# Strassen output products behind the attention: two interleaved groups of 192-column products, or one group of 384-column products per token pair

## The chip, the cores and the metric

One core of one Trainium2 chip. The metric is the device time of one execution in microseconds (us); the time before is the median of three runs. Engines are named as in the profile: PE (TensorE matmul), PEld (TensorE weight load), DVE (VectorE), ACT (ScalarE), POOL (GpSimd), SP (SyncE, which here only issues transfers).

## The reference

Softmax attention over 8 batches, 12 heads, 448 tokens and head size 64, followed by a SwiGLU block on the 3584 x 768 result:

```python
scores = scale * np.matmul(q, k.transpose(0, 1, 3, 2))
attn = np.exp(scores - np.max(scores, axis=-1, keepdims=True))
attn = attn / (np.sum(attn, axis=-1, keepdims=True) + 1e-09)
x = np.matmul(attn, v).transpose(0, 2, 1, 3).reshape(B * S, H * D)      # 3584 x 768
g = x @ w_gate                                                           # 768 x 1536
return (g * (1.0 / (1.0 + np.exp(-g))) * (x @ w_val)) @ w_out            # 1536 x 768
```

The change concerns only the last product, hidden (3584 x 1536) times w_out (1536 x 768).

## The kernel before

Everything is emitted in an order written out by hand. The attention runs over pairs of heads; the blocks of the SwiGLU (384 or 512 tokens of a pair of batches) are interleaved with it, so that PE always has something to do while ACT makes the exponentials. Behind the attention, from about 300 us on, PE alone sets the pace. What is left there is, in order of time: the gate and value products of a 512-token block by a seven-product (Strassen) scheme (`Unit`, L833); the output products of the three token pairs that are still open (`run_groups`, the groups named `og`, L710); the gate and value products of the last two batches, again by `Unit`, with the output of one odd 128-token chunk in between (`single_out`, L1039); and the output products of the last three token pairs (again `run_groups` and `og`, L710), with the stores that end the kernel.

**The output product of a token pair.** A token pair is 256 tokens, two chunks x and y of 128. Its hidden values have 12 chunks of 128 features, in two halves of NH = 6, so the left operand has four blocks: A11, A12 (chunk x) and A21, A22 (chunk y). The right operand is split into row halves and two column groups of equal width. Seven products of six matmuls each replace the eight of the plain form. Four sums of w_out's blocks (`Tsum`, made by `out_sums` on DVE during the attention) and four sums of the hidden blocks (`h_sums`, L571 to L574, four operations on DVE for each token pair) are operands.

In `out_group` the column groups are the two 192-column quarters of one 384-column half of w_out (`QW` = 192, `OH` = 384), so a token pair takes two groups, `qw` = 0 and 1, of seven products of 192 columns. The sums `Tsum` pair the same quarters. A group takes one tile of two PSUM banks from the pool `ps_s` (three such tiles; the pool `ps_f` has two tiles of one bank): `a` and `c` share the first bank and `b` has the second. The order of the seven products on PE is a, c, b, b, a, c, b:

1. `a` and `c` receive the first two products. Then ACT copies `a` to p1 (L756), and DVE makes p15 = c/HS + p1 (L757).
2. `b` receives the third product, and DVE writes c = HS * p15 + b (L759).
3. `b` receives the fourth, and DVE takes from it the right quarter of row y (`part`, L763).
4. `a` and `c` receive the fifth and sixth, and ACT copies both to row x in one operation of 384 columns (L735).
5. `b` receives the seventh, and DVE takes from it the left quarter of row y (L773).

The generator yields after step 2, and `run_groups` runs the two groups of a token pair interleaved: group one's first stage, group two's first stage, group one's second, group two's second. While one group's copies run, PE is in the other's products. `add_sum` takes the next waiting DVE operation from the list `sums`: four to a token pair, at places between the stages. The list holds `h_sums` of the next token pairs, and behind the first three pairs also `token_sums` (L1028 to L1031), four larger sums for the last `Unit` stage.

The two rows of a token pair are stored from SP's queue in parts (`store`, L671). The very last token pair stores in smaller parts as they become ready, from the queues of SP and ACT in turn.

Of the kernel before, what the change touches and what calls it, by code (L numbers as in the profile page):

```python
# [16 lines left out]
HS = 4096.0  # L17
# [48 lines left out]
def kernel(  # L66
# [487 lines left out]
    def out_sums(c):  # L554
        b11, b12, b21, b22 = (
            wo_all[:, :, ds(f, 2), ts(i, QW)].rearrange("p h c m -> p c h m") for f in (c, NH + c) for i in range(2)
        )
        t1, t2, t3, t4 = (t[:, ds(c, 2)].rearrange("p c (h m) -> p c h m", h=2) for t in Tsum)
        return [
            lambda: nc.vector.tensor_sub(t1, b12, b11),  # L560
            lambda: nc.vector.tensor_sub(t2, b22, t1),
            lambda: nc.vector.tensor_sub(t3, b22, b12),
            lambda: nc.vector.tensor_sub(t4, b21, t2),
        ]
# [137 lines left out]

    def out_group(kk, c0, hts, t, at, qw, osb, last=False, own=False, mid=None):
        x, y, w = ts(2 * t, 128), ts(2 * t + 1, 128), ts(qw, QW)
        g = ps_s.tile([128, 2, 512], FP32, tag="s", name="og")
        a, c, b = g[:, 0, 0:QW], g[:, 0, QW:OH], g[:, 1, 0:QW]

        def product(dst, lhs, rhs, first=False):
            return [
                nc.tensor.matmul(  # L710
                    dst, lhsT=lhs(n), rhs=rhs(n), start=first and n == 0, stop=n == NH - 1, skip_group_check=True
                )
                for n in range(NH)
            ]

        def hh(half, z):
            return lambda n: hts[:, half * NH + n, z]

        def hs(m):
            return lambda n: Hall[at][m][:, n]  # L720

        def bb(oh, half):
            return lambda n: wo[qw][:, half * NH + n, ts(oh, QW)]

        def tt(m):
            return lambda n: Tsum[m][:, n, w]

        def out_part(z, src):
            if last and qw:
                halves = [osb[z][:, ds(qw * OH + x * QW, QW)] for x in range(2)]  # L730
                return [
                    nc.scalar.activation(halves[0], src[:, 0:QW], AF.Copy, scale=1.0 / HS),
                    nc.vector.tensor_scalar_mul(halves[1], src[:, QW:], 1.0 / HS),
                ]
            return [nc.scalar.activation(osb[z][:, ts(qw, OH)], src, AF.Copy, scale=1.0 / HS)]  # L735

        def stored(z, lo=0, w=OH):
            l0 = c0 + (2 * t + z) * 128
            if last:
                store(osb[z], kk, l0, 128, qw * OH + lo, w, (nc.sync, nc.scalar), True)  # L740
            elif qw and not lo:
                store(osb[z], kk, l0, 128, 0, DM)

        def apart(mms, *others):
            for mm in mms:
                for other in others:
                    tc.declare_no_dep(mm.ins, other.ins, reason="another bank")

        product(a, hh(0, x), bb(0, 0), True)
        product(c, hh(0, y), tt(0))  # L750
        p1 = fp.tile([128, QW], FP32, tag="p1", name="p1")
        p15 = fp.tile([128, QW], FP32, tag="p15", name="p15")
        if own:
            keep1 = nc.vector.tensor_scalar_mul(p1[:], a, 1.0 / HS)
        else:
            keep1 = nc.scalar.activation(p1[:], a, AF.Copy, scale=1.0 / HS)  # L756
        keep15 = nc.vector.scalar_tensor_tensor(p15[:], c, 1.0 / HS, p1[:], ALU.mult, ALU.add)  # L757
        apart(product(b, hs(0), tt(1), True), keep1, keep15)
        nc.vector.scalar_tensor_tensor(c, p15[:], HS, b, ALU.mult, ALU.add)  # L759
        yield  # L760
        product(b, hs(1), tt(2))
        d = osb[1][:, ds(qw * OH + QW, QW)]
        part = nc.vector.scalar_tensor_tensor(d, b, 1.0 / HS, p15[:], ALU.mult, ALU.add)  # L763
        if last:
            stored(1, QW, QW)
        if mid:
            mid()
        apart(product(a, hh(1, x), bb(0, 1)), part)
        apart(product(c, hs(2), bb(1, 1)), part)
        row0 = out_part(0, g[:, 0, 0:OH])  # L770
        stored(0)
        apart(product(b, hh(1, y), tt(3)), *row0)
        nc.vector.scalar_tensor_tensor(osb[1][:, ds(qw * OH, QW)], b, 1.0 / HS, p1[:], ALU.mult, ALU.add)  # L773
        stored(1, 0, QW if last else OH)
        yield

# [145 lines left out]
    with tc.manual_schedule():  # L922
# [49 lines left out]

        def pair_groups(kk, c0, hts, t, last=False, at=None):
            at = t if at is None else at
            osb = []

            def begin(qw, own=False, mid=None):
                if not qw:
                    osb.extend(new_osb() for _ in range(2))
                return out_group(kk, c0, hts, t, at, qw, osb, last, own, mid)  # L980

            return [(lambda own=False, mid=None, qw=qw: begin(qw, own, mid), h_sums(hts, t, at) if not qw else []) for qw in range(2)]

        def add_block(i, visits):
            if i < B - NB - 1:
                f1, own, n = block(i)
                fvq.extend(f1)
                kk, c0, hts = own
            else:
                own = None  # L990
            t_out = NFB * OH / 2400.0
            if i == 0:
                oq.extend([(ffn2_steps(*own, by_half(range(n // 128), OH)), t_out)] * (2 * (n // 128)))
            if i < 2:
                if i:
                    ffn2_wait.append(own)
                    sums.extend(wsums)
                    wsums.clear()
                return
            kk, c0, hts = ffn2_wait.pop()  # L1000
            ffn2_wait.append(own)
            odd = i % 2 == 0
            groups.extend(x for t in range(1 + odd) for x in pair_groups(kk, c0, hts, t))
            if not odd:
                w = QW
                oq.extend([(ffn2_steps(kk, c0, hts, by_half([2], w)), t_out)] * (DM // w))
            sums.extend(groups[0][1])
            later = [f for _, fs in groups[1:] for f in fs]
            groups[:] = [(begin, []) for begin, _ in groups]
            sums.extend(later)  # L1010


# [82 lines left out]
        def run_o():  # L1095
# [7 lines left out]
            return t  # L1103

        def run_group(nf, inside=None, gate_first=False, sum_between=True):
            gen = groups.pop(0)[0](gate_first)
            for _ in range(nf - 1):
# [18 lines left out]
        def run_group_with(p0):  # L1126
            gen = groups.pop(0)[0](True, lambda: pv_close(p0, 1))
            next(gen)
            pv_pieces(p0)
            pv_close(p0, 0)  # L1130
            next(gen)
            turn_x(p0)

        def run_two_groups(inside=None):
            gens = [groups.pop(0)[0]() for _ in range(2)]
            for stage in range(2):
                for gen in gens:
                    next(gen)
                if inside and not stage:
                    inside()  # L1140

# [267 lines left out]
        for u in range(6, NFB):  # L1409
            items[f"W_{u}"] = (POOL_, 3.65, [f"W_{u - 1}"], lambda u=u: weight_sums(u))  # L1410
        groups5 = [pair_groups(KL - 1, 384, hts5, t, at=1 - t) for t in range(2)]
        sums.clear()
# [6 lines left out]

        def run_groups(pairs):  # L1420
            for pair in pairs:
                one, two = (begin(mid=add_sum) for begin, _ in pair)
                next(one)
                add_sum()
                for gen in (two, one, two):
                    next(gen)
                add_sum()

        x7 = X[KL]
        t7 = token_space(xp.tile([128, NCB, NT], FP16, tag="X", name="T")[:].rearrange("p a b -> p (a b)"), S)  # L1430
        tsums7 = token_sums(x7, S, t7)
        first, behind = (pair[0][1] for pair in groups5)
        first[0]()
        sums.extend([tsums7[0], *first[1:], *behind, *tsums7[1:]])
        for pair in [groups] + groups5:
            run_groups([pair])

# [4 lines left out]
        Hall[2] = [h[:, 0 : NH * 128].rearrange("p (c f) -> p c f", c=NH) for h in Hall[2]]  # L1442
        final = [pair_groups(KL, 0, hts, t, t == 2) for t in range(3)]
        ops = []
# [6 lines left out]
        for half in range(2):  # L1451
            for f in range(NFB):
                after = [f"F{f % 2}1_{f // 2 * 2 + 1}", f"O{half}_{f - 1}" if f else f"F10_{NFB - 2 + half}"]
                items[f"O{half}_{f}"] = (PE_, OH / 2400 + 0.0025, after, lambda half=half, f=f: single_last(half, f))
        for m, fn in enumerate(final[0][0][1]):
            u = NFB - 1 if m else NH - 1
            items[f"H{m}"] = (DVE_, 0.65, [f"F00_{u}", f"F10_{u}"] + [f"H{m - 1}"] * (m > 0), fn)
        run_items(items)

        sums.extend(f for pair in final[1:] for _, fs in pair for f in fs)  # L1460
        run_groups(final)


# [28 lines left out]
```

## Time and profile before

| | |
|---|---|
| median of three runs | 427.54 us (427.53 to 427.55) |
| the profiled execution: own time, span | 427.29 us, 425.5 us |
| PE, DVE, ACT, POOL busy, share of the span | 99%, 64%, 58%, 54% |
| granted PE clock | 1.00 in every stretch |
| matmuls | 4796, of them 924 in `og` (L710) |
| of these 924, behind 327.5 us | 504, in two stretches: 327.5 to 348.3 us and 400.3 to 421.3 us |

The span is the traced execution from its first instruction to its last; the own time is the same execution's device time, 1.79 us longer. A matmul's row gives a duration that includes its way through the array (246 ns for 192 columns, 326 ns for 384); consecutive matmuls overlap, so the pace of PE is read from the starts and not from the durations.

### The profile page before, as it was taken

The page shows a single profiled execution, that of the slowest core. Times are in us where ns is not written, and L with a number is a line of the kernel's source. Part 1 is how long each engine was busy: PE and PEld are TensorE (multiplying, and loading weights), DVE is VectorE, ACT ScalarE, POOL GpSimd, SP SyncE. Part 2 cuts the span into 40 slices and gives each one's busy share as a digit, 9 for nine tenths or more (in the row PEclk, how much of TensorE's full clock was granted, in tenths as well). Part 3 has the DMA queues.
Part 4 walks back from the last instruction along what each step waited for, and adds up shares of the span by engine and source line. Part 5 has one row for each costly group of instructions (what it writes and reads, how often), then busy time and mean ns, then how long its engine had stood idle before and what let it go on. Part 6 is the DMA issues. An engine that isn't in the chain of part 4 may idle for free.

```text
span 425.5 us, 11944 instructions
## 1 busy us (share of the span) xinstructions
PE 419.2 (99%) x4796; PEld 292.0 (69%) x4796; DVE 271.1 (64%) x644; ACT 244.9 (58%) x395; POOL 229.8 (54%) x351
## 2 busy tenths in 40 slices
PE   8999999999999999999999999999999999999996
PEld 3766666655557777757766777777889985555795
DVE  4666572785669656575635776677777765665663
ACT  6975667646755654656666546559654235545221
POOL 8656614997887774468733876935999000000000
PEclk9999999999999999999999999999999999999999
DMA  9999999999999999999999998723101231000125
GB/s 136 182 200 200 199 175 190 136 177 215 115 138 143 124 176 121 141 146 129 119 148 136 151 144 106 139 46 94 23 2 29 87 114 36 0 2 1 39 75 149
DMA packets 107928, 49.79 MB, mean 117 GB/s; under 512 B 59872, under 2 KB 104672, under 8 KB 107872
## 3 DMA queue, kind: packets, MB, share of 16 engines
q0 software_dynamic: 46800, 24.56, 52.3%
q1 hardware_dynamic: 60752, 24.22, 30.9%
q8 instruction: 37, 0.61, 0.6%
q10 hardware_dynamic: 320, 0.25, 0.2%
q14 instruction: 19, 0.16, 0.1%
HBM read 49.55 MB, written 11.01 MB: 142 GB/s over the span
## 4 chain that ended last, share of the span: by engine, by line
PE 92%; ACT 4%; DVE 2%; DMA 0%; issue 0%; ACTq 0%; DVEq 0%
PE og L710 17%; PE gp L588 17%; PE vp L588 12%; PE un L833 10%; PE acc L438 8%; PE ub L833 8%; PE s L346 5%; PE op L681 5%; PE acc L402 2%; PE s L376 2%; ACT E L366 2%; PE s L358 1%; ACT E L384 1%; PE tp L317 1%; PE wp L164 1%; PE op L1039 1%
## 5 line engine op out<-in xcount | busy, mean ns | idle before, releaser
L366 ACT ACTIVATE E<-s 128x896 f16<-128x896 f32 x126 | 106.6, 918 | 40.2 <-PE s L346 28.3
L588 PE MATMUL gp<-X,wg 128*128 128x384 f16 (+1 forms) x360 | 74.0, 347 | 0.0
L238 POOL COPY qk<-qkraw 128x512 f16<-128x512 f16 x70 | 43.4, 666 | 55.2 <-DMA qkT<-qk 55.0
L588 PE MATMUL vp<-X,wv 128*128 128x384 f16 (+3 forms) x360 | 66.7, 321 | 0.1
L641 DVE SCALAR_TENSOR_TENSOR t<-sg,gp 128x384 f32<-128x384 f32 (+1 forms) x60 | 36.1, 607 | 41.7 <-ACT sg L615 41.6
L588 PEld LDWEIGHTS <-wv 128*128 128x128 f16 x462 | 43.7, 98 | 25.8 <-issue 0.3
L588 PEld LDWEIGHTS <-wg 128*128 128x128 f16 x360 | 32.8, 98 | 26.2 <-issue 1.9
L178 POOL DMA_DIRECT2D vraw<-in_v_dram x72 | 44.3, 643 | 9.4 <-DVE X L523 8.5
L615 ACT ACTIVATE sg<-gp 128x384 f32<-128x384 f32 (+1 forms) x60 | 32.1, 537 | 27.9 <-PE gp L588 27.4
L178 POOL DMA_DIRECT2D qkraw<-in_k_dram x70 | 42.8, 631 | 6.5 <-DMA wo<-in_moe_w_out_dram 4.0
L384 ACT ACTIVATE E<-s 112x896 f16<-112x896 f32 x48 | 40.5, 917 | 7.9 <-PE s L376 7.8
L438 PEld LDWEIGHTS <-E 128*128 128x128 f16 (+2 forms) x1224 | 38.0, 98 | 10.1 <-issue 4.0
L710 PEld LDWEIGHTS <-hts 128*128 128x128 f16 x528 | 44.1, 98 | 0.3
L438 PE MATMUL acc<-vo,E 128*128 128x65 f16 (+2 forms) x1224 | 42.4, 193 | 0.1
L647 DVE SCALAR_TENSOR_TENSOR hts<-t,vp 128x384 f16<-128x384 f32 (+3 forms) x60 | 32.5, 541 | 5.8 <-PE vp L588 1.9
L481 DVE TENSOR_TENSOR xt<-acc,R 128x256 f16<-128x256 f32 x72 | 30.6, 425 | 2.5
L735 ACT ACTIVATE osb<-og 128x384 f32<-128x384 f32 x21 | 10.3, 490 | 37.9 <-PE og L710 37.9
L201 POOL DMA_DIRECT2D qkraw<-in_q_dram x43 | 29.6, 688 | 4.3 <-DMA vraw<-in_v_dram 1.4
L346 PE MATMUL s<-qkT 64*64 64x448 f16 (+1 forms) x288 | 30.8, 354 | 0.4
L710 PE MATMUL og<-wo,hts 128*128 128x192 f16 x264 | 29.0, 246 | 0.0
L710 PEld LDWEIGHTS <-hsum 128*128 128x128 f16 x300 | 25.6, 98 | 1.0
L219 DVE COPY vo<-vraw 128x512 f16<-128x512 f16 (+1 forms) x48 | 21.8, 457 | 3.0 <-DMA vraw<-in_v_dram 2.9
(184 smaller groups left out, 708.8 us busy)
## 6 DMA issues: line engine op xcount, KB each, us to landing
vraw<-in_v_dram POOLq DMA_DIRECT2D x72, 64.0 KB, 4.9
qkraw<-in_q_dram POOLq DMA_DIRECT2D x39, 112.0 KB, 4.2
qkraw<-in_k_dram POOLq DMA_DIRECT2D x68, 64.0 KB, 4.7
wg<-in_moe_w_gate_dram POOLq DMA_DIRECT2D x8, 288.0 KB, 9.8
wv<-in_moe_w_val_dram POOLq DMA_DIRECT2D x8, 288.0 KB, 10.4
wo<-in_moe_w_out_dram POOLq DMA_DIRECT2D x2, 1152.0 KB, 19.2
out_dram<-osb SPq DMA_DIRECT2D x7, 288.0 KB, 3.7
out_dram<-osb SPq DMA_DIRECT2D x6, 336.0 KB, 3.4
```

The costliest lines, as they stand in the source:

```text
L178: eng.dma_start(dst[ts(s, 64)], rows)
L238: nc.gpsimd.tensor_copy(dst.rearrange("p c h d -> p h c d"), src)
L346: nc.tensor.matmul(s[ts(half, m), hx, 0:S], lhsT=t[ts(hx, 64), ds((c + low(pr, hx)) * 128 + half * m, m)], rhs=t[ts(hx, 64), ds(NC * 128, S)],
L366: nc.scalar.activation(e[:, 0 : 2 * S].rearrange("p (h q) -> p h q", h=2), s[:, :, 0:S], AF.Exp, scale=sm_scale)
L384: nc.scalar.activation(e[:, :, 0:S], s[0:P, :, 0:S], AF.Exp, scale=sm_scale)
L438: nc.tensor.matmul(acc[ds(lo, m), ts(j, D + 1)], lhsT=e[rows, ds(hx * S + j * 128 + lo, m)], rhs=Vts[pr % NV][rows, hx, col, 0 : D + 1], s ...
L588: nc.tensor.matmul(dst[:, 0:w], lhsT=wslice(kind, self.fb, cb), rhs=X[kk][:, cb, ds(c0 + lo, w)], start=(cb == 0), stop=(cb == NCB - 1),)
L615: self.readers = [nc.scalar.activation(self.sg[:, 0:n], gp[:, 0:n], AF.Tanh, scale=0.5)]
L641: nc.vector.scalar_tensor_tensor(self.t1[:, 0:n], self.sg[:, 0:n], 1.0, self.gp[:, 0:n], ALU.add, ALU.mult)
L647: nc.vector.scalar_tensor_tensor(self.hts[:, self.fb, ds(lo, w)], self.t1[:, ds(lo, w)], 0.5 * HS, vp[:, 0:w], ALU.mult, ALU.mult)
L710: nc.tensor.matmul(dst, lhsT=lhs(n), rhs=rhs(n), start=first and n == 0, stop=n == NH - 1, skip_group_check=True)
L833: mm = nc.tensor.matmul(dst, lhsT=lhs[:, n], rhs=rhs[:, n], start=first and n == 0, stop=n == NK - 1, skip_group_check=True,)
```

## The change

The sums of w_out now pair the two 384-column halves: `wo[0]` with `wo[1]`, instead of the two quarters within each half. A class `OutPair` replaces `out_group` and `pair_groups`. Its method `narrow` is the former group for use during the attention: the same seven products of 192 columns, with `qw` choosing the quarter within both halves, and one ACT copy that writes two strips of 192 columns. Its method `wide` is one group for a whole token pair: seven products of 384 columns, with `a` and `c` in the two banks of one `ps_s` tile and `b` in a `ps_f` tile, and p1 and p15 in the buffers `kept`. `run_wide` runs the wide groups one behind the other, in both stretches behind the attention. The last token pair's seventh product is made in two parts of 256 and 128 columns, each with its own DVE operation and stores.

```diff
     def out_sums(c):
-        b11, b12, b21, b22 = (
-            wo_all[:, :, ds(f, 2), ts(i, QW)].rearrange("p h c m -> p c h m") for f in (c, NH + c) for i in range(2)
-        )
-        t1, t2, t3, t4 = (t[:, ds(c, 2)].rearrange("p c (h m) -> p c h m", h=2) for t in Tsum)
+        b11, b12, b21, b22 = (wo[i][:, ds(f, 2)] for f in (c, NH + c) for i in range(2))
+        t1, t2, t3, t4 = (t[:, ds(c, 2)] for t in Tsum)
...
+        def narrow(self, qw, own=False, mid=None):
+            osb, lo = self.open(), qw * QW
...
+            row0 = nc.scalar.activation(
+                osb[0][:].rearrange("p (h m) -> p h m", h=2)[:, :, ds(lo, QW)],
+                g[:, 0, 0:OH].rearrange("p (h m) -> p h m", h=2),
+                AF.Copy,
+                scale=1.0 / HS,
+            )
...
+        def wide(self, keep, add_sum):
+            osb = self.open()
+            g = ps_s.tile([128, 2, 512], FP32, tag="s", name="og")
+            b = ps_f.tile([128, 512], FP32, tag="f", name="ob")[:, 0:OH]
+            a, c = g[:, 0, 0:OH], g[:, 1, 0:OH]
+            p1, p15 = (k[:, 0:OH] for k in keep)
+            both = (nc.sync, nc.scalar)
+            product(a, self.hh(0, self.x), self.bb(0, 0, 0, OH), True)
+            product(c, self.hh(0, self.y), self.tt(0, 0, OH), True)
+            nc.scalar.activation(p1, a, AF.Copy, scale=1.0 / HS)
+            keep15 = nc.vector.scalar_tensor_tensor(p15, c, 1.0 / HS, p1, ALU.mult, ALU.add)
+            add_sum()
+            product(b, self.hs(0), self.tt(1, 0, OH), True)
+            part = nc.vector.scalar_tensor_tensor(c, p15, HS, b, ALU.mult, ALU.add)
+            add_sum()
+            apart(product(a, self.hh(1, self.x), self.bb(0, 1, 0, OH)), keep15, part)
+            left = nc.scalar.activation(osb[0][:, 0:OH], a, AF.Copy, scale=1.0 / HS)
+            tc.declare_no_dep(left.ins, part.ins, reason="another bank")
+            if self.last:
+                self.stored(0, 0, OH, both)
+            product(b, self.hs(1), self.tt(2, 0, OH))
+            nc.vector.scalar_tensor_tensor(osb[1][:, OH:], b, 1.0 / HS, p15, ALU.mult, ALU.add)
+            if self.last:
+                self.stored(1, OH, OH, both)
+            add_sum(2)
+            apart(product(c, self.hs(2), self.bb(1, 1, 0, OH)), left)
+            nc.scalar.activation(osb[0][:, OH:], c, AF.Copy, scale=1.0 / HS)
+            if self.last:
+                self.stored(0, OH, OH, both)
+            else:
+                self.stored(0)
+            for lo, w in ((0, 256), (256, 128)) if self.last else ((0, OH),):
+                product(b[:, ds(lo, w)], self.hh(1, self.y), self.tt(3, lo, w))
+                nc.vector.scalar_tensor_tensor(
+                    osb[1][:, ds(lo, w)], b[:, ds(lo, w)], 1.0 / HS, p1[:, ds(lo, w)], ALU.mult, ALU.add
+                )
+                if self.last:
+                    self.stored(1, lo, w, both)
+            if not self.last:
+                self.stored(1)
...
-        def run_groups(pairs):
-            for pair in pairs:
-                one, two = (begin(mid=add_sum) for begin, _ in pair)
-                next(one)
-                add_sum()
-                for gen in (two, one, two):
-                    next(gen)
-                add_sum()
+        def run_wide(pairs):
+            for n, pair in enumerate(pairs):
+                pair.wide(kept[2 * (n % 2) : 2 * (n % 2) + 2], add_sum)
...
-        for pair in [groups] + groups5:
-            run_groups([pair])
+        run_wide([groups[0][0], *groups5])
...
-        run_groups(final)
+        run_wide(final)
```

More of the change, by code (lines that the diff above doesn't have):

```diff
@@ L701, in ffn2_steps @@
             yield
[L703 to L711, printed above, removed]
-                )
[L713 to L775, printed above, removed]
@@ L971 @@
         steps = []
[L973 to L982, printed above, removed]
         def add_block(i, visits):
@@ L1002, in add_block @@
             odd = i % 2 == 0
-            groups.extend(x for t in range(1 + odd) for x in pair_groups(kk, c0, hts, t))
+            new = [OutPair(kk, c0, hts, t) for t in range(1 + odd)]
+            groups.extend((pair, qw) for pair in new for qw in range(2))
             if not odd:
@@ L1006, in add_block @@
                 oq.extend([(ffn2_steps(kk, c0, hts, by_half([2], w)), t_out)] * (DM // w))
[L1007 to L1010, printed above, removed]
+            for pair in new:
+                sums.extend(pair.sums())
         FIRST_STEPS = [2, 2, 1, 2, 1, 1, 1]
@@ L1103, in run_o, with next_group @@
             return t
+        def next_group(*args):
+            pair, qw = groups.pop(0)
+            return pair.narrow(qw, *args)
         def run_group(nf, inside=None, gate_first=False, sum_between=True):
-            gen = groups.pop(0)[0](gate_first)
+            gen = next_group(gate_first)
             for _ in range(nf - 1):
@@ L1126, in run_group_with @@
         def run_group_with(p0):
-            gen = groups.pop(0)[0](True, lambda: pv_close(p0, 1))
+            gen = next_group(True, lambda: pv_close(p0, 1))
             next(gen)
@@ L1132, in run_group_with @@
             turn_x(p0)
[L1134 to L1137, printed above, removed]
-                    next(gen)
-                if inside and not stage:
-                    inside()
         def run_budget(budget):
@@ L1410 @@
             items[f"W_{u}"] = (POOL_, 3.65, [f"W_{u - 1}"], lambda u=u: weight_sums(u))
-        groups5 = [pair_groups(KL - 1, 384, hts5, t, at=1 - t) for t in range(2)]
+        groups5 = [OutPair(KL - 1, 384, hts5, t, 1 - t) for t in range(2)]
         sums.clear()
@@ L1418 @@
         run_items(items)
-        def run_groups(pairs):
-            for pair in pairs:
-                one, two = (begin(mid=add_sum) for begin, _ in pair)
-                next(one)
-                add_sum()
-                for gen in (two, one, two):
-                    next(gen)
-                add_sum()
+        def run_wide(pairs):
+            for n, pair in enumerate(pairs):
+                pair.wide(kept[2 * (n % 2) : 2 * (n % 2) + 2], add_sum)
         x7 = X[KL]
@@ L1431 @@
         tsums7 = token_sums(x7, S, t7)
-        first, behind = (pair[0][1] for pair in groups5)
+        first, behind = (pair.sums() for pair in groups5)
         first[0]()
         sums.extend([tsums7[0], *first[1:], *behind, *tsums7[1:]])
-        for pair in [groups] + groups5:
-            run_groups([pair])
+        assert [qw for _, qw in groups] == [0, 1] and groups[0][0] is groups[1][0]
+        run_wide([groups[0][0], *groups5])
         hts = hview(0, NT)
@@ L1442 @@
         Hall[2] = [h[:, 0 : NH * 128].rearrange("p (c f) -> p c f", c=NH) for h in Hall[2]]
-        final = [pair_groups(KL, 0, hts, t, t == 2) for t in range(3)]
+        final = [OutPair(KL, 0, hts, t, last=t == 2) for t in range(3)]
         ops = []
@@ L1454 @@
                 items[f"O{half}_{f}"] = (PE_, OH / 2400 + 0.0025, after, lambda half=half, f=f: single_last(half, f))
-        for m, fn in enumerate(final[0][0][1]):
+        for m, fn in enumerate(final[0].sums()):
             u = NFB - 1 if m else NH - 1
@@ L1458 @@
         run_items(items)
-        sums.extend(f for pair in final[1:] for _, fs in pair for f in fs)
-        run_groups(final)
+        sums.extend(f for pair in final[1:] for f in pair.sums())
+        run_wide(final)
 _INS = ['q', 'k', 'v', 'moe_w_gate', 'moe_w_val', 'moe_w_out']
```

59 lines of the change are left out of this document (added).

## The prediction

> **What bounds the kernel now.** I read the page first: PE is busy all the time, and the chain that ended last is made of its products, those of `og` (L710) in front.
>
> ```profile
> PE 419.2 (99%) x4796; PEld 292.0 (69%) x4796; DVE 271.1 (64%) x644; ACT 244.9 (58%) x395; POOL 229.8 (54%) x351
> ...
> PE 92%; ACT 4%; DVE 2%; DMA 0%; issue 0%; ACTq 0%; DVEq 0%
> ```
>
> The built programs of both kernels, laid side by side, differ on the engines only behind 327 us, apart from ten ACT copies that write two strips of 192 instead of one of 384. So two stretches count; the windows of the trace are cut there (columns: length, busy time with number of instructions for PE, PEld, DVE, ACT and POOL, granted PE clock, DMA share, GB/s).
>
> ```profile
> 327.50:348.30 20.80, 20.80 (x255) 20.79 (x253) 15.40 (x36) 4.94 (x13) 1.23 (x2) 1.00 0.33 96
> ...
> 400.30:421.30 21.00, 20.98 (x254) 20.72 (x251) 11.68 (x31) 5.18 (x13) 0.00 (x0) 1.00 0.37 112
> 421.30:425.50 4.20, 0.00 (x0) 0.00 (x0) 0.62 (x2) 0.07 (x1) 0.00 (x0) 1.00 0.33 98
> ```
>
> PE does not pause in either `og` stretch: no copy is ever late. Every pause that the change brings is therefore new time, and so is every matmul cost it saves. Third, the start of the last stretch in the timeline (start, duration, engine), which gives the latencies:
>
> ```profile
> 400.32 0.66 PE L710 MATMUL og<-wo,hts 128*128 128x192 f16 x6
> 400.82 0.66 PE L710 MATMUL og<-E,hts 128*128 128x192 f16 x6
> ...
> 401.31 0.66 PE L710 MATMUL og<-E,hsum 128*128 128x192 f16 x6
> 401.51 0.33 ACT L756 ACTIVATE p<-og 128x192 f32<-128x192 f32 x1 [0.50 <-PE og L710]
> ...
> 401.81 0.66 PE L710 MATMUL og<-wo,hts 128*128 128x192 f16 x6
> 401.87 0.36 DVE L757 SCALAR_TENSOR_TENSOR p<-og,p 128x192 f32<-128x192 f32 x1 [2.19 <-ACT p L756]
> 402.30 0.66 PE L710 MATMUL og<-E,hts 128*128 128x192 f16 x6
> 402.34 0.36 DVE L759 SCALAR_TENSOR_TENSOR og<-p,og 128x192 f32<-128x192 f32 x1
> 402.61 0.55 DVE L571 TENSOR_TENSOR qkraw<-hts 128x768 f16<-128x768 f16 x1
> ```
>
> The chain product c, ACT copy, two DVE operations ends at 402.70, while b's own group wants it back only at 402.80: group two's three products lie between. A wide group has one product there. Fourth, the durations by shape (count, busy time, mean ns of one, idle before):
>
> ```profile
> L641 DVE SCALAR_TENSOR_TENSOR t<-sg,gp 128x384 f32<-128x384 f32 x36 | 19.7, 553 | 20.7 <-ACT sg L615 20.7
> ...
> L573 DVE TENSOR_TENSOR hsum<-hts 128x768 f16<-128x768 f16 x10 | 5.5, 552 | 0.1
> ...
> L1028 DVE TENSOR_TENSOR T<-X 128x1344 f16<-128x1344 f16 x1 | 0.9, 852 | 0.0
> ```
>
> **What is saved: matmuls.** Products of six 192-column matmuls start 0.495 us apart (41 of them from 400.32 to 420.62), 82.5 ns a matmul. Matmuls of 384 columns take 162.4 ns (12 of `gp` in 1.95 us on the chain of waits). Each stretch has 3 pairs: 252 x 82.5 = 20.79 us before, 126 x 162.4 = 20.46 after: 0.33 us saved in each.
>
> **What is added: a wait in every wide group.** I call its products a1, c1, b1, a2, b2, c2, b3; each lasts 0.974 us (6 x 162.4). In the built program p1's copy waits for c1's last matmul, not a1's: the p15 operation, which reads `c`, names only ACT among its waits, so ACT's wait must cover c1. b2's first matmul waits for the DVE operation that reads `b` (`part`). From the group's start:
>
> - c1's last matmul starts at 0.974 + 5 x 0.1624 = 1.79. A reader begins 0.36 later (326 ns for 384 columns, plus the 0.03 between 401.48 and 401.51): p1 at 2.15. It lasts 0.49 (L735, 384 columns), and DVE follows 0.03 later: p15 at 2.67.
> - p15 lasts 0.553 (L641). Then `add_sum` puts another operation ahead of `part`. On DVE an independent follower starts 0.08 to 0.09 before the end (402.61 against 402.70). For `h_sums` (0.55) `part` starts at 2.67 + 0.47 + 0.47 = 3.61, ends at 4.17, and PE goes on 0.05 later (as at 28.71 us of the trace, behind a DVE cast, L523, that ended at 28.66): 4.22. PE has been free since a2's end, 4 x 0.974 = 3.90: **0.32 us lost**.
> - For `token_sums` of the last batches (L1028 to L1031, 0.85) it is 0.30 more: **0.62 lost**.
> - With no sum, `part` starts 0.11 after p15's end (L757 to L759), so b2 at 3.94: **0.04 lost**.
>
> The first stretch has token_sums, h_sums, token_sums in that place: 0.62 + 0.32 + 0.62 = 1.56, less 0.33: **+1.23**. The last has h_sums, h_sums, none: 0.32 + 0.32 + 0.04 = 0.68, less 0.33: +0.35 for the end of its sixth product.
>
> Costed at nothing: b3's wait for the right-half operation on `b` (ready 1.17 + 0.55 + 0.05 = 1.77 us after b2's start, needed at 1.95; c2 covers it with 0.18 to spare, and a DVE operation longer by more than that costs its excess in each group); osb buffers and `kept`, whose last readers end over 1 us before; the strided ACT copies, off PE's path; SP and POOL keep their order.
>
> **The end.** b3 of the last pair comes in 256 and 128 columns, and the second part waits for DVE's reading of the first, the same tile. b3 starts at 400.32 + 21 x 0.974 - 0.974 + 0.68 = 419.80 + 0.68 = 420.48. The first part's last matmul starts 0.55 later (109 ns each), its result is read from 421.33 on, for 0.42 (L647, 256 columns); PE resumes at 421.80, its last matmul starts 0.28 later, and the last DVE operation runs from 422.33 for 0.29 (0.352 at 192 less 64 x 1.05 ns) to 422.62. Before:
>
> ```profile
> 420.62 0.66 PE L710 MATMUL og<-qkraw,hts 128*128 128x192 f16 x6
> ...
> 421.41 0.36 DVE L733 TENSOR_SCALAR osb<-og 128x192 f32<-128x192 f32 x1 [1.22 <-DMA out_dram<-osb]
> 421.68 0.35 DVE L773 SCALAR_TENSOR_TENSOR osb<-og,p 128x192 f32<-128x192 f32 x1
> 421.80 0.85 ACTq L671 DMA_DIRECT2D out_dram<-osb  x2
> ```
>
> The last DVE operation ended at 422.03, 0.59 earlier. But the last two stores were then issued only at about 422.2 and 422.27, behind two of 120 and 72 KB issued at 421.80, and landed 2.1 us later; stores of 72 and 24 KB alone (418.3) took 1.7 and 1.8. After, the last ones are of 48 and 16 KB, leave at 422.65 from idle queues, 0.9 us behind the ones before: 1.8 us taken, 1.6 to 2.1 as bounds. Landing at 424.45 against 424.37, and the span ends 1.13 later: 425.58 against 425.50. The last stretch and the end together: **+0.08** (-0.12 to +0.4).
>
> **Sum.** +1.23 + 0.08 = +1.31 us: the profiled execution's 427.29 becomes 428.60, and the median, 0.25 above it, 427.54 + 1.31 = 428.85. About 0.2%, 0.86 us here, is what a measurement of this kernel can tell from no change.
>
> **Bounds.** The DVE operations on f32 in `kept` and two banks are unseen; the nearest rows, 0.553 and the in-place 0.363 against 0.356, make them 0.55 to 0.57. With 0.05 us either way in each of six stalls the sum moves 0.3 us; with the end's bounds it is +0.8 to +2.0.
>
> **Rivals.** *The first copy is not held* (not slower). Each accumulator has a bank of its own in the wide group, so p1 could run after a1, at 1.17, and p15 at c1's end, 2.70. `part` then starts at 3.12 (h_sums) or 3.39 (token_sums), and only the two token_sums groups lose 0.10. First stretch 0.20 - 0.33 = -0.13; the end comes 0.68 earlier, +0.08 - 0.68 = -0.60: 427.54 - 0.73 = 426.81. What decides is whether p1 starts before 2.15 in its group. Against it stands p15's missing wait for PE; 0.05. The Trainium skill, "PSUM — Partial Sum Buffer", section "PSUM bank collisions raise a hardware error", says that waits are needed by bank and quadrant only, by which this rival would be open to the hardware. The trace of before cannot show it, as `a` and `c` share a bank there and p1 starts (401.51) after c's product in every group.
>
> *A second wait opens*: b3 behind the right-half operation, if DVE falls 0.2 us or more further behind than worked out. Six groups at 0.1 to 0.3 us on top: 429.4 to 430.6. For it: DVE is 74% busy in the first stretch. Against: 0.18 us of room, and fewer DVE operations (one of 384 for two of 192). 0.06.
>
> *Stalls half as long*, because DVE overlaps or starts sooner than its rows say, and a tail that lands early: 1.56 + 0.68 halved gives +1.31 - 1.12 = +0.19, 427.7. DVE's starts in the rows repeat within 0.02 us, which speaks against it. 0.06.
>
> *The clock falls in the pauses*: a lower granted clock in both stretches, say 0.81, would add 41 x 0.23 = 9.6 us. The page grants 1.00 even in the opening, where PE is busy 4.00 of 5 us. 0.01. The Trainium skill, "TensorE: Matmul & The Clock Gate", section on the second failure mode ("psum-queue depth-cycling"), warns of frequent short idles while cycling through banks; no row here shows it.
>
> That the change does not do what it says has no room: in the built program 504 matmuls of 192 columns have given way to 120 of 384, six of 256 and six of 128.
>
> **Numbers.** The forecast has 0.82. The range 428.2 to 429.7 takes in nearly all of that (its bounds give 428.34 to 429.5, widened a little for errors in the latencies that all six waits share) and the lower end of the second wait. Slower by over 0.2% (above 428.40): 0.76 of the forecast, the second wait and the clock, 0.83. Within 0.2%: 0.06 of the forecast, the half stalls, and 0.02 of the unheld copy, which lies near the edge of 426.68: 0.14. Faster: the other 0.03 of that copy.
>
> **What would show it.** In the timeline of after: six waits of PE on DVE, one in each wide group ahead of b2, of about 0.6, 0.3, 0.6, 0.3, 0.3 and 0.04 us; p1's copy 2.15 us after its group's start; products 0.97 us apart elsewhere; a gap of 0.6 us inside b3 of the last pair, and its last stores issued near 423.9 on the new time axis. If the stretches take 20.5 us without gaps, the wait was wrongly read; if gaps stand ahead of b3, DVE was.

## The result: slower by half a per cent, and the profile after

The changed kernel takes 429.77 us (median; 428.84 to 431.58), against 427.54 us before in the same comparison (427.1 to 428.03): 1.0055 times the time before, with a 95% interval of 1.0043 to 1.0067. Two later comparisons of the same two kernels gave 1.0033 (1.002 to 1.0046) and 1.0036 (1.0023 to 1.005). The forecast was 428.85, with a range up to 429.7: the sign and the mechanism held, and the time lies 0.07 us above the range.

The profiled execution of after has a span of 427.0 us and an own time of 428.84 us, 1.55 more than that of before. The page, its line of engines and the line of the chain by engine:

```profile
PE 418.9 (98%) x4550; PEld 275.3 (64%) x4550; DVE 266.3 (62%) x620; ACT 244.0 (57%) x389; POOL 229.9 (54%) x351
...
PE 89%; ACT 4%; DVE 3%; issue 1%; DMA 1%; SPq 0%; DVEq 0%; ACTq 0%
```

PE has 246 matmuls fewer, and its share of the chain is 89%, where before had 92%. The windows of after, cut at the first `og` product behind the attention, at the first product of the last `Unit` stage, and at the first `og` of the last stretch (length, busy time and instructions of PE, PEld, DVE, ACT and POOL, granted clock, DMA share, GB/s):

```profile
327.29:349.48 22.19, 20.96 (x129) 12.31 (x127) 13.66 (x24) 4.62 (x10) 1.15 (x2) 1.00 0.30 89
349.48:401.43 51.95, 51.95 (x280) 27.19 (x279) 31.22 (x53) 25.48 (x49) 0.00 (x0) 1.00 0.05 17
401.43:424.00 22.57, 21.23 (x133) 12.62 (x131) 10.58 (x21) 4.90 (x10) 0.00 (x0) 1.00 0.37 111
424.00:427.00 3.00, 0.00 (x0) 0.00 (x0) 0.00 (x0) 0.00 (x0) 0.00 (x0) 1.00 0.27 81
```

PE is now idle for 1.2 us of the first stretch and 1.3 of the last (0.4 of these behind its last matmul, which ends at 423.61), at a granted clock of 1.00. The view of PE's waits from 327 us on names the cause (us in total, times, longest):

```profile
PE ob L703 <- DVE og L793: 1.7, 5, 0.5
PE ob L703 <- DVE osb L813: 0.5, 1, 0.5
```

L793 is `part`. PE's products of `b` wait for it in five of the six groups, and once, at the very end, for the reading of b3's first 256 columns. (These idle times count from the modelled end of the product before; the waits below count from where the next product would have started, which is 0.16 us earlier.)

One wide group in the timeline, the first of the last stretch (start, duration, engine):

```profile
401.43 1.14 PE L703 MATMUL og<-wo,hts 128*128 128x384 f16 x6
402.40 1.14 PE L703 MATMUL og<-E,hts 128*128 128x384 f16 x6
...
403.64 0.49 ACT L789 ACTIVATE kept<-og 128x384 f32<-128x384 f32 x1 [1.52 <-PE og L703]
404.16 0.56 DVE L790 SCALAR_TENSOR_TENSOR kept<-og,kept 128x384 f32<-128x384 f32 x1 [3.38 <-ACT kept L789]
...
404.63 0.55 DVE L569 TENSOR_TENSOR qkraw<-hts 128x768 f16<-128x768 f16 x1
405.10 0.56 DVE L793 SCALAR_TENSOR_TENSOR og<-kept,ob 128x384 f32<-128x384 f32 x1
...
405.71 1.14 PE L703 MATMUL ob<-E,hsum 128*128 128x384 f16 x6 [0.22 <-DVE og L793]
```

a1 and c1 start at 401.43 and 402.40. p1's copy starts only at 403.64, behind c1; then come p15, a sum for the next pair, and `part`; b2 starts at 405.71, 4.28 after the group's start, where four products at 0.975 would have put it at 3.90. Over the six groups the waits ahead of b2 (its start less that of a2, less 0.975) are 0.67, 0.365 and 0.675, then 0.385, 0.385 and 0.095 us.

The end of the kernel in the same view:

```profile
421.78 0.82 PE L703 MATMUL ob<-qkraw,hts 128*128 128x256 f16 x6
...
422.64 0.42 DVE L813 SCALAR_TENSOR_TENSOR osb<-ob,kept 128x256 f32<-128x256 f32 x1 [1.07 <-PE ob L703]
423.11 0.50 PE L703 MATMUL ob<-qkraw,hts 128*128 128x128 f16 x6 [0.52 <-DVE osb L813]
423.65 0.29 DVE L813 SCALAR_TENSOR_TENSOR osb<-ob,kept 128x128 f32<-128x128 f32 x1 [0.59 <-PE ob L703]
```

b3's two parts stand 0.5 us apart with DVE between them, and the last DVE operation ends at 423.94, 3.06 before the span's end (before: 422.03 and 3.47).

**How times are compared below.** From run to run the time of one kernel scatters by 0.9 to 4.6 us. In the ten traces what differs beyond the kernels' own stretches lies in the opening, which is the same code in all these kernels (last section). So each experiment is also read by its *tail*, from the first `og` product behind the attention to the end of the span. Of that, the first stretch ends with the first product of the last `Unit` stage, 51.95 us lie between the two stretches in every trace of before and after and in every experiment within 0.01, and the rest is the last stretch with the end.

| kernel | first stretch | last stretch and end | tail | median us | ratio (95%) |
|---|---|---|---|---|---|
| before | 20.79 | 25.18 | 97.92 | 427.54 | |
| after | 22.19 | 25.57 | 99.71 | 429.77 | 1.0055 (1.0043 to 1.0067) |
| e1_again | 22.19 | 25.56 | 99.70 | 429.64 | 1.0033 (1.002 to 1.0046) |
| e2_early | 20.81 | 24.76 | 97.52 | 427.31 | 0.9985 (0.9968 to 1.0002) |
| e3_sums | 20.78 | 25.04 | 97.77 | 427.85 | 0.9988 (0.9976 to 1.0) |
| e4_narrow | 20.79 | 25.34 | 98.08 | 428.13 | 1.0002 (0.9984 to 1.0019) |
| e5_both | 20.48 | 24.71 | 97.14 | 427.41 | 0.9978 (0.9961 to 0.9994) |
| e6_banks | 20.48 | 24.60 | 97.03 | 427.48 | 0.9985 (0.9974 to 0.9997) |
| e7_whole | 20.48 | 24.89 | 97.31 | 427.41 | 0.9981 (0.997 to 0.9993) |
| e8_again | 22.19 | 25.51 | 99.65 | 429.8 | 1.0036 (1.0023 to 1.005) |

The runs e1 to e4 stand against before's 428.19 us in their own comparison, e5 to e8 against 427.98. By the tail the change costs +1.79, +1.78 and +1.73 us in three traces of after, while by the medians it is 2.23, 1.45 and 1.82. The spans are printed to 0.1 us, so a tail is good to about 0.05; with the unrounded spans that the traces hold (425.496 us for before, 426.992, 429.300 and 427.041 for after) the cost is 1.78, 1.78 and 1.77: the code's own cost repeats.

The times expected of e2, e3 and e4 were missed by 0.3 to 0.7 us in the median, each on the slow side; their tails came out as expected. In the profiled executions the openings make the difference: there the first `og` product behind the attention starts 0.4 to 0.9 us later than in after's trace.

### The profile page after: what moved, and what is told of

It is laid out like the page before. It is cut to its first block, busy times and chain, and to the rows that moved or that the text cites. A ratio compares the mean times of both kernels' runs of the same rounds, so it can differ in the third digit from the quotient of the medians.

```text
span 427.0 us, 11383 instructions
## 1 busy us (share of the span) xinstructions
PE 418.9 (98%) x4550; PEld 275.3 (64%) x4550; DVE 266.3 (62%) x620; ACT 244.0 (57%) x389; POOL 229.9 (54%) x351
## 4 chain that ended last, share of the span: by engine, by line
PE 89%; ACT 4%; DVE 3%; issue 1%; DMA 1%; SPq 0%; DVEq 0%; ACTq 0%
PE gp L586 16%; PE vp L586 12%; PE og L703 12%; PE un L877 10%; PE ub L877 8%; PE acc L438 8%; PE s L346 5%; PE op L679 5%; PE ob L703 3%; PE acc L402 2%; PE s L376 2%; ACT E L366 2%; DMA out_dram<-osb 1%; ACT E L384 1%; PE s L358 1%
## 5 line engine op out<-in xcount | busy, mean ns | idle before, releaser
L703 PEld LDWEIGHTS <-hts 128*128 128x128 f16 x390 | 34.3, 98 | 9.8 <-issue 0.7
L703 PE MATMUL og<-wo,hts 128*128 128x192 f16 (+1 forms) x192 | 26.8, 276 | 0.0
L703 PEld LDWEIGHTS <-hsum 128*128 128x128 f16 x216 | 19.5, 98 | 8.3 <-issue 2.1
L480 DVE RECIPROCAL R<-acc 128x4 f32<-128x4 f32 x72 | 12.6, 176 | 17.6 <-PE acc L438 17.5
L219 DVE COPY vo<-vraw 128x512 f16<-128x512 f16 (+1 forms) x48 | 19.4, 406 | 3.8 <-DMA vraw<-in_v_dram 3.7
```

Source lines behind the costliest of these rows:

```text
L703: nc.tensor.matmul(dst, lhsT=lhs(n), rhs=rhs(n), start=first and n == 0, stop=n == NH - 1, skip_group_check=True)
```

## The experiments

**e1_again and e8_again: the changed kernel, unaltered,** one with each set.

> The changed kernel as it is, once more. The profiled execution of it (428.84 us) lay 1.55 us above the one of before (427.29), but the median of its seven runs 2.23 above (429.77, from 428.84 to 431.58). Theory A: all of the steady difference is the six waits of PE on DVE, about 1.6 us, and the rest is a scatter that the pauses bring: the granted clock was 0.998 to 0.999 in four of the seven runs. Then this kernel scatters again by 1 us and more above 428.8, and the kernels without pauses do not. Theory B: the scatter belongs to the chip or to the run. Then the kernel before and all four kernels of this call scatter alike, and this one stays 1.5 to 1.6 us above before.

> The changed kernel once more, for its distance from before. Two comparisons gave 2.2 us (429.77 against 427.54) and 1.45 us (429.64 against 428.19), while the traces have 1.79 us from the first product behind the attention to the end, the same in both traces of it (99.7), and an opening that differs by up to 2.3 us between executions of one and the same code. Theory A: the distance is 1.8 us, and the rest of both figures is the opening's scatter; expected 1.4 to 2.2. Rival: the change makes the opening longer too, and the distance is 2.2 or more.

Measured: 429.64 and 429.8 us, tails 99.70 and 99.65. The cost in the tail is firm; what differs between the traces lies ahead of the first stretch, in code that the change does not touch. Theory B of e1_again holds: before and the kernels without these pauses scatter as widely (before 427.23 to 430.4 us, e2_early 426.85 to 429.7, e3_sums 426.94 to 428.64, e4_narrow 427.06 to 430.58). Nor do the granted clocks of 0.998 and 0.999 come from the pauses where a trace can tell: in e3_sums, e5_both and e7_whole the trace's own list of clock intervals, of which the granted clock in the views is a mean, has full speed up to 1.1 to 1.3 us before the span's end, behind PE's last matmul, and half speed only from there. For e8_again, 1.82 us by the medians lies in the expected 1.4 to 2.2.

**e2_early: p1's copy is no longer held by c1.** The copy is emitted ahead of product c, and c's matmuls are declared independent of it (another bank).

```diff
 product(a, self.hh(0, self.x), self.bb(0, 0, 0, OH), True)
-product(c, self.hh(0, self.y), self.tt(0, 0, OH), True)
-nc.scalar.activation(p1, a, AF.Copy, scale=1.0 / HS)
+keep1 = nc.scalar.activation(p1, a, AF.Copy, scale=1.0 / HS)
+apart(product(c, self.hh(0, self.y), self.tt(0, 0, OH), True), keep1)
```

> One wait taken away: p1 is copied by ACT right behind the first product, and the second product, which goes to the other bank, does not wait for that copy. p1 starts about 1.2 us after its group's start instead of 2.21, p15 at 2.73 at the latest, when the second product is done. Theory A: part then starts at about 3.15 (h_sums ahead) or 3.45 (token_sums), so only the two groups with token_sums keep a wait, of 0.1 to 0.2 us; 1.7 - 0.3 = 1.4 us less in the first stretch and the end 0.7 us earlier, in all 2.0 to 2.2 us below the changed kernel's own profiled execution, 426.7 to 427.0. Rival: the DVE operation put ahead of part is what makes the wait, wherever p1 stands; then less than 0.7 us is won.

Measured: 427.31 us, tail 97.52, 2.19 shorter than after's. The timeline of e2_early, the same group as above:

```profile
400.44 1.14 PE L703 MATMUL og<-wo,hts 128*128 128x384 f16 x6
...
401.67 0.49 ACT L788 ACTIVATE kept<-og 128x384 f32<-128x384 f32 x1 [0.54 <-PE og L703]
...
402.66 0.56 DVE L790 SCALAR_TENSOR_TENSOR kept<-og,kept 128x384 f32<-128x384 f32 x1 [2.86 <-PE og L703]
...
404.34 0.49 PE L703 MATMUL ob<-E,hsum 128*128 128x384 f16 x2
```

The copy starts 1.23 after the group, beside product c, and p15 now waits for PE's c1 (the releaser in its brackets is PE, in after it was ACT) and starts at 2.22 instead of 2.73. b2 starts at 3.90, with no wait. What is left ahead of b2 is 0.17 us in each of the two groups with `token_sums`. So taking away the wait for c1 on p1's copy is enough to turn the loss into a gain of 0.40 us in the tail; the median cannot tell e2 from before (0.9968 to 1.0002).

**e3_sums: nothing between p15 and `part`.** The first `add_sum` goes, and its operation runs behind the right-half operation instead.

```diff
 keep15 = nc.vector.scalar_tensor_tensor(p15, c, 1.0 / HS, p1, ALU.mult, ALU.add)
-add_sum()
 product(b, self.hs(0), self.tt(1, 0, OH), True)
...
-add_sum(2)
+add_sum(3)
```

> The other half of the chain: p1 waits for the second product as in the changed kernel, but no sum stands between the p15 operation and part; it is made behind the fourth product instead. Theory A: every one of the six waits shrinks to that of the last group, which has no sum (0.10 us in the trace): 0.67 + 0.36 + 0.67 + 0.38 + 0.38 become 5 x 0.1, 2.0 us less, about 426.9 to 427.2 against 428.84. Rival (only the copy's wait counts): the waits stay at 0.3 us or more each, 427.9 and up.

Measured: 427.85 us, tail 97.77, 1.94 shorter than after's. p1's copy starts as late as in after; each wait is about 0.10 us. The DVE operation in between is thus the larger part of each wait (0.3 of 0.4 us with `h_sums`, nearly 0.6 of 0.67 with `token_sums`). e2 and e3 do not add up: either one takes away nearly all of the wait, since PE only waits for what exceeds its next product.

**e4_narrow: only the last pair is wide.** The five other pairs behind the attention are emitted as two interleaved groups of 192 columns, as before the change.

```diff
 for n, pair in enumerate(pairs):
+    if not pair.last:
+        one, two = (pair.narrow(qw, mid=add_sum) for qw in range(2))
+        next(one)
+        add_sum()
+        for gen in (two, one, two):
+            next(gen)
+        add_sum()
+        continue
     pair.wide(kept[2 * (n % 2) : 2 * (n % 2) + 2], add_sum)
```

> All token pairs behind the attention but the very last one go as two interleaved groups of 192 columns again, on the new pairing of halves; the last pair stays one wide group with its split seventh product. What the new pairing and the new strips cost in themselves is left. Theory A: both stretches lose their pauses and their saving of 2.4 ns a matmul; against the kernel before there remain only the last group and the end, -0.1 to +0.3 us: 427.4 to 427.8, without scatter. Rival: the pairing costs something in the attention (the DVE sums of the weights, the strided ACT copies), and the kernel stays 0.5 us or more above before.

Measured: 428.13 us, tail 98.08, 0.16 above before's. The first stretch is before's again (20.79), with no wait: the new pairing of w_out's halves and the strided ACT copies cost nothing. Nor does the attention with the new narrow groups take longer: from its first `og` product to the last `op` matmul it is 193.6 us in after and in before. The 0.16 are the wide last pair and its end alone.

**e5_both: e2 and e3 together.**

> Both edits at once: p1 is copied behind the first product without holding the second, and no sum stands ahead of part. Theory A (the six waits are all that the wide groups cost): no wait is left ahead of b2, 126 wide matmuls take 20.5 us in each stretch, the first stretch is 0.3 us shorter than before's 20.79, and from the first product behind the attention to the end of the span it takes 97.1 us, against 97.92 before, 99.71 in the changed kernel, 97.52 with the early copy alone. Rival: another wait takes the place of the one removed (b3 behind the right-half operation, now that the sums are bunched behind it), and it stays at 97.5 or above. Of the opening, whose length differs from run to run in the traces so far, the time inherits a scatter of 1 us and more; so the stretch counts more than the median, which should lie 0.6 to 1.0 us below before's.

Measured: 427.41 us, 0.57 below before's median where 0.6 to 1.0 were expected; tail 97.14, as expected (97.1), 0.78 below before's. The window of its first stretch:

```profile
328.96:349.44 20.48, 20.48 (x129) 12.33 (x126) 13.61 (x24) 4.63 (x10) 1.17 (x2) 1.00 0.33 97
```

PE does not pause, and the stretch takes 20.48 us against 20.79 before: this is the pure saving of 126 matmuls of 384 columns in place of 252 of 192, 0.31 us. The only wait left behind the attention is b3's 0.5.

**e6_banks: e5, and the last pair's `b` in two tiles of `ps_f`,** 256 and 128 columns, so that b3's second part need not wait for the reading of the first. The last pair's b1 and b2, and the DVE operations that read them, come in two parts each as well.

```diff
-b = ps_f.tile([128, 512], FP32, tag="f", name="ob")[:, 0:OH]
+cuts = ((0, 256), (256, 128)) if self.last else ((0, OH),)
+bs = [(ps_f.tile([128, 512], FP32, tag="f", name="ob")[:, 0:w], lo, w) for lo, w in cuts]
...
-for lo, w in ((0, 256), (256, 128)) if self.last else ((0, OH),):
-    product(b[:, ds(lo, w)], self.hh(1, self.y), self.tt(3, lo, w))
+for b, lo, w in bs:
+    product(b, self.hh(1, self.y), self.tt(3, lo, w))
```

> As the one with both edits, and in the last token pair the accumulator b lies in two tiles of a bank each, 256 and 128 columns, so that the second part of the seventh product does not wait for DVE's reading of the first part (0.52 us of pause inside b3 in the changed kernel, 2.16 us from b3's start to the end of the last DVE operation). Theory A: that becomes 1.5 us, but the stores of the two parts then follow each other closely on their queues, so 0.2 to 0.5 us of the 0.66 reach the end. Rival: the end hangs on the stores of 120 and 72 KB issued earlier, and nothing is won.

Measured: 427.48 us, tail 97.03, the shortest. PE has no wait at all behind the attention. From b3's start to the end of the last DVE operation it takes 1.48 us instead of 2.15, but the tail shrinks by only 0.11 against e5: from the last DVE operation to the end of the span it is 3.59 us instead of 3.06, near before's 3.47. The last stores, of 48 and 16 KB, took 1.9 and 2.0 us to land, where they took 1.8 and 1.7 in e5; that accounts for 0.1 to 0.3 of the 0.53 given back, and where the rest lies the view of the transfers does not say. That is less than the 0.2 to 0.5 us expected to reach the end, and more than the rival's nothing.

**e7_whole: e5, and the last pair's seventh product in one piece.**

```diff
-for lo, w in ((0, 256), (256, 128)) if self.last else ((0, OH),):
+for lo, w in ((0, OH),):
```

> As the one with both edits, but the last token pair's seventh product is whole: one product of 384 columns, one DVE operation, one pair of stores of 144 and 48 KB. From b3's start to the end of the last DVE operation 1.73 us instead of 2.16, but the last stores are three times as large: they took 2.1 to 2.2 us in the traces where the small ones took 1.7. Theory A: the two cancel, within 0.15 us of the kernel with both edits. Rival: the wait inside b3 counts in full, and the whole product ends 0.4 us earlier.

Measured: 427.41 us, tail 97.31, 0.17 longer than e5's (0.15 by the unrounded spans; within 0.15 was expected, and the rival's 0.4 the other way is out). Without the cut there is no wait inside b3, and from b3's start to the end of the last DVE operation it is 1.74 us instead of 2.15, but the last stores are one of 144 and one of 48 KB, and land in 2.3 and 2.2 us. By the tail of one trace each, the cut with its wait is still the better one, and the cut in two banks better again.

e5, e6 and e7 are all faster than before, by 0.5 to 0.6 us in the medians and by 0.6 to 0.9 in the tail. Among the three the medians cannot tell (427.41, 427.48, 427.41); the tail puts e6 first, by 0.11 us (0.12 unrounded) in one trace each.

## Where the prediction was right and where it was not, step by step

**The mechanism held.** p1's copy waits for c1, `part` comes behind a sum, PE waits for `part` ahead of b2 in every wide group, in the order large, small, large, small, small, none: 0.62, 0.32, 0.62, 0.32, 0.32, 0.04 forecast, 0.67, 0.365, 0.675, 0.385, 0.385, 0.095 measured. e2 and e3, which take away one link each, show that both links are needed for the wait.

**In the sum, the term that was mis-sized is the release of p1's copy.** The step "A reader begins 0.36 later (326 ns for 384 columns, plus the 0.03 between 401.48 and 401.51)" gave p1 at 2.15; it starts at 2.21. The chain of waits of after shows where the 0.06 lie (start, us, what):

```profile
401.59 1.96 PE og L703 x12
403.55 0.02 issue
403.57 0.02 ACTq L789
403.59 0.04 issue
403.64 0.50 ACT kept L789
```

c1 ends at 403.55, 2.12 after the group's start, as worked out (1.79 + 0.326), but from there to the copy it is 0.09 and not 0.03: a step of ACT's queue stands between two short ones. The copy may wait there for more than one semaphore; that is a reading of the order of these steps, not shown by a run of its own. It does not hang on c1: in e2 the copy, which of the products waits for a1 alone, also starts 0.09 behind the end of its product (401.58 and 401.67). All that follows went as forecast: p15 0.52 behind p1, `part` 0.94 behind p15 with `h_sums`, PE 0.05 behind `part`. So all six waits are longer by the same 0.045 to 0.065. The bounds had nearly that in them ("0.05 us either way in each of six stalls"); the waits came out at their upper edge.

**The sum.** First stretch: waits 1.71 for 1.56, saving 0.31 (e5) for 0.33, together +1.40 for +1.23. Last stretch and end: waits 0.865 for 0.68, b3's start 0.19 later than forecast; b3 to the last DVE operation 2.16 for 2.14; from there to the span's end 3.06 for 2.96, though the last stores landed in 1.7 us, at the fast end of the forecast's 1.6 to 2.1; what took the 0.10 more, the view of the transfers does not say. Together +0.39 for +0.08. The tail: +1.79 for +1.31, within the forecast's bounds of +0.8 to +2.0.

**The step that put the time outside the range is the median's offset.** The step "the median, 0.25 above it" carried before's offset between profiled execution and median over to after. After's median lies 0.93 above its profiled execution. The three runs of before that were at hand agreed within 0.02 us, and the range was made for the code's cost alone; +1.79 on 427.54 would be 429.33, inside the range. By the three traces of after, whose tails agree, the other 0.44 us of the measured 429.77 are not in the stretches that the change touches. They fit the scatter of the opening, as the two repeats of the comparison (1.45 and 1.82 us) suggest; no execution at the median has a trace that would show it. The repeats also show on which side the offset lay: after's median hardly moved (429.64, 429.8), while before's was 428.19 and 427.98, 0.4 to 0.7 us above the 427.54 on which the forecast was built. Whether that first figure stood low by chance or by the chip that it ran on, the record does not show.

**The rivals.** *The first copy is not held*: not so in this build, but e2 shows what it would have been: four of the six waits gone, and the tail 0.40 below before's where the rival's sum gave 0.73. Its condition, p1 ahead of 2.15, was the right one. Its working has a slip, p15 "at c1's end, 2.70", where its own further figures (`part` at 3.12, 0.94 behind p15) follow from 2.18; measured, 2.22, 0.10 behind c1's end as above, so the `token_sums` groups lose 0.17 each and not 0.10. The Trainium skill, "PSUM — Partial Sum Buffer", section "PSUM bank collisions raise a hardware error", needs waits by bank and quadrant only; e2 agrees, its copy reads one bank while PE writes the next and starts 1.23 us after its group. *A second wait opens* at b3: no, PE's waits list only `part` and the cut inside the last b3. *Stalls half as long*: no, they are longer. *The clock falls in the pauses*: the granted clock is 1.00 in all four windows, the trace's list of clock intervals has full speed without a break from 4.72 us to behind the span's end, and the 20 us with three pauses ran at 0.975 us a product between them, as without pauses. The Trainium skill's warning on this ("TensorE: Matmul & The Clock Gate", section "A second HAM failure mode: psum-queue depth-cycling") is not borne out by pauses this short, 0.1 to 0.7 us, and this rare, six in 42 us of products. The forecast's price for this rival rests on an assumed clock of 0.81, which no trace here has (the lists know 1.0 and 0.5 only), and 41 x 0.23 is 9.4, not 9.6. The argument against it, that the page grants 1.00 even in the opening, does not hold: before's list of clock intervals has no entry until 5.71 us, and the page prints 1.00 where there is none (last section).

**What the prediction costed at nothing** held: the strided copies and the new pairing (e4's first stretch at 20.79), b3's wait for the right-half operation, the buffers, the order on SP and POOL.

## What to carry to other kernels

Two interleaved groups hide the latency from a product through two engines and back to the accumulator; merging them into one wide group halves the matmuls, but gains only what fewer matmuls save (0.31 us in 20.79 here) and exposes the latency, so count the products that lie between a bank's last write and its next one before widening, and keep optional work out of that chain on the engine that closes it. When an instruction waits for a later product than the one that it reads, look whether it carries the wait for its follower: emitting it a product earlier was worth 2.2 us of the tail here and turned a loss into a gain. And when before's runs agree within 0.02 us, that says nothing of the scatter of other runs: a range for a median needs room for it, on the side of the time before as well.

## What the hardware showed that was not expected

**The opening scatters by itself, and a granted clock of 1.00 there need not be a measurement.** The first `og` product behind the attention starts between 327.29 and 329.60 us in the ten traces, and the attention's own first `og` product between 133.3 and 135.6; from there to the last `op` matmul ahead of the first stretch it is 193.6 or 193.7 us in every trace. In e1_again, the latest, PE stayed at its slow pace for longer. Four of the 448-column score matmuls and the warm-up matmuls (`wp`) in the timeline, of after and then of e1_again (start, duration):

```profile
5.00 0.39 PE L164 MATMUL wp<-warm 128*128 128x512 f16 x1
5.79 0.55 PE L376 MATMUL s<-qkT 64*128 64x448 f16 x4 [0.40 <-DVE qkT L301]
```

```profile
8.64 0.61 PE L164 MATMUL wp<-warm 128*128 128x512 f16 x1
9.18 0.93 PE L376 MATMUL s<-qkT 64*128 64x448 f16 x4
...
10.66 0.55 PE L376 MATMUL s<-qkT 64*128 64x448 f16 x4
```

After is fast from 5.0 us on, e1_again still slow at 9.2 and fast only by 10.7; its first `acc` product starts at 12.66 us, after's at 10.77. The windows of both read a granted clock of 1.00 all the way. The list of clock intervals in the packed trace, of which the windows print a mean, says otherwise: its first entry, full speed, begins 4.72 us into the span in after and 10.24 in e1_again (5.71 in before, 4.48 to 6.92 in the other seven), and ahead of its first entry the windows count full speed. The durations agree with the list: in before a `wp` matmul takes 0.61 us at 5.20 and 0.39 at 6.30. So the slow start is recorded, and the 1.00 ahead of it stands only for a missing entry. The Trainium skill, "TensorE: Matmul & The Clock Gate", Part 1, has a gate that opens after about 3.4 us of work, in a window that runs free of the kernel's start, and calls the length of the slow start run-variable; the traces agree in that, but e1_again's start is longer by over 5 us, more than one such window. In e1_again alone PE paused for 0.18 us ahead of a `tp` matmul at 5.07; whether that kept the clock low for longer, no run shows. In other traces (e3, e5, e7) the opening was late without that: PE has waits of 0.2 to 0.9 us there that before and after do not have, some for early loads, some for which the view names no releaser.

**A shorter finish moves the end by less.** Taking 0.67 us out of the last products and DVE operations (e6 against e5) moved the end by 0.11 us, and making it 0.41 us shorter by leaving out the cut, with larger last stores (e7 against e5), moved it by 0.17 us the other way. In these two comparisons, of one trace each, what was gained in front of the last stores was for the most part, or more than wholly, given back behind the last DVE operation.
